# First requests on three queues, and a gate row in four column tiles

## Chip, core and metric

The kernel runs on one core of one Trainium2 chip. The metric is the device time of one execution in microseconds (us). Before the change the median of three runs is 543.81 us (543.6 to 544.0).

The core has TensorE (PE, with its weight loads shown as PEld), VectorE (DVE), ScalarE (ACT), GpSimd (POOL) and SyncE (SP). SP, ACT and POOL can each issue DMA transfers on a queue of their own. Each engine works through its instructions in the order in which the program lists them.

## What is computed

One transformer block on x of 2048 rows and 576 columns, modulated by a condition vector c of 576 values:

```python
mod = (silu(c) @ w_mod).reshape(1, 6, 1, 576)
sa, ca, ga, sb, cb, gb = mod[:, 0], ..., mod[:, 5]
h = layernorm(x) * (1 + ca) + sa
x = x + ga * A(h)       # 32 heads of 18, each row attends to 8 rows, 2 apart, then wo
h = layernorm(x) * (1 + cb) + sb
x = x + gb * ((h @ w_gate) * (h @ w_up)) @ w_down      # 4608 hidden columns
```

The six modulation rows depend on c alone. The rows `ga` and `gb` (here the attention gate row and the MLP gate row) multiply whole columns of the output, so they are needed on all 128 partitions; the other four are needed as columns.

## The kernel before

The 2048 rows are cut into eight chunks of 256. The MLP works on groups of chunks, `[0], [1, 2], [3, 4], [5, 6], [7]`. For each group there is a gate-up loop (36 steps, one per 128 hidden columns, TensorE products `pg` and `pu` at L706) and a down loop (`acc` at L921, `accr` at L926). Attention of the coming chunks is interleaved with these loops. Chunk 0, chunk 1 and part of chunk 2 run ahead of the first gate-up loop, in an opening whose order is written out by hand; this opening lasts about 49 us.

**The opening.** The program asks for the transfers in this order. ACT's queue: `c_row`, the vector c, in three requests (L185, L187). SP's queue: the two halves of chunk 0 of x (L203), the two "tails" of the modulation weights `wmA` (the last 64 of the 576 contraction rows, L190), the two main parts of `wmA` (L206), then the QK and V weights (L174, L175), chunk 1 of x (L136), the weights `wmC` of the attention gate row (L180, L181) and more. TensorE first runs filler matmuls (`keep_busy`, L196: seven of 512 columns), then transposes c (`pc`, L1029), runs seven more fillers, and computes the first two modulation rows as columns (`mod_columns`, L321). These products use four column tiles: four matmuls with 32 columns of weights each write four 32-partition strips of one bank (L328). Between them stand the transposes of the normalised x (L313). ACT copies the result (L332), it is transposed again and added (L342, L345), the transposed x is modulated (L302, L304), and the first QK products follow (L416).

POOL spends the opening on memsets and masks, the identity matrix among them (L221, L222), and issues few transfers.

**The gate rows.** `mod_row` (L349) computes a gate row on all 128 partitions at once: the weights are the condition vector repeated 128 times (`sc_bc`), and five matmuls of 512 columns (`pa`) and five of 64 (`pb`) accumulate over the five parts of the contraction; ACT copies both to an f32 tile. It runs once for the attention gate in the opening (`wmC`) and once for the MLP gate (`gb_row`, L1257) in the first gate-up loop. The weights of the second one are loaded by `load_wm5` (L1015) on POOL's queue, into a spare part of the tile `hh` and a tile `wm5r` from the pool of output tiles (named `o_t` in the profile). `gb_row` then asks on POOL's queue for block 3 of `w_down` (`ld_d1`, L1252, which also lands in a spare part of `hh`). The row is used from the end of the first down loop on, near 127 us (L949, L954, L996).

**The first gate-up loop.** Its weights come in blocks of four steps (`load_wgu`, L154; block 3 is also kept in a spare part of `hh`, so the profile shows it as `hh<-in_B_w_up_dram`). What is interleaved is placed by a planner (`timed`, L808). It gets threads of pieces, each with a cost on TensorE, a cost on DVE, the marks that it needs, the mark that it sets and a delay after which the mark counts; it keeps a clock and puts a piece after the first step at which its marks are due. It also places the QK and V products of chunk 3 as pairs of row tiles (`qkv_of`). Chunk 3's layer norm (`norm_of`, L683) is normalised on ACT (`norm_act`, L283, ACT's work at L287): per half of the chunk one instruction of 576 columns, and one of 64 that repeats the last columns. The chunk is then transposed by DMA on SP's queue (`a_td`, L391, `hT<-xn`) and modulated (`a_mod`).

Of the kernel before, what the change touches and what calls it, by code (L numbers as in the profile page):

```python
# [7 lines left out]
BF = mybir.dt.bfloat16  # L8
# [10 lines left out]
P = 128  # L19
D = 576  # L20
# [6 lines left out]
DIL = 2  # L27
FF = 4608
FT = FF // P
HALO = 16  # L30
SPAN = 14
EPS = 1e-5
# [12 lines left out]
def kernel(  # L45
# [55 lines left out]
    eps = consts.tile([P, 1], F32, name="eps")  # L101
    modc = consts.tile([P, 4, KT], F32, name="modc")
    ga_bc = consts.tile([P, D], F32, name="ga_bc")
    gb_bc = consts.tile([P, D], F32, name="gb_bc")
    sc_bc = consts.tile([P, KT, P], BF, name="sc_bc")
    xns = [consts.tile([P, ST, DP], BF, name=f"xn{k}") for k in range(2)]
    o_sb = consts.tile([P, ST, DP], BF, name="o_sb")
# [5 lines left out]
    wv = wts.tile([P, KT, D], BF, name="wv")  # L113
    wo = wts.tile([P, KT, D], BF, name="wo")
    vd = dramp.tile([HALO + S, D], BF, name="vd")
    prod_t = consts.tile([P, 4 * KT * CH], BF, name="prod_t")
    prod_n = [0]

# [63 lines left out]

    wmA = sp.tile([P, KT, 2 * D], BF, name="wmA")
    c_row = sp.tile([KT, P], BF, name="c_row")
    nc.scalar.dma_start(c_row[0:KF, :], c[0, 0:KF * P].rearrange("(m p) -> m p", p=P))  # L185
    for c0 in (0, 64):
        nc.scalar.dma_start(c_row[KF:KT, c0:c0 + 64], c[:, KF * P:D])  # L187
    def load_wm_tail(wm, blk):
        for b in range(2):
            nc.sync.dma_start(wm[64 * b:64 * (b + 1), KF, b * D:(b + 1) * D], w_mod[KF * P:D, (blk + b) * D:(blk + b + 1) * D])  # L190

    maskneg = sp.tile([P, W, H], BF, name="maskneg")
    busy_w = sp.tile([P, NB], BF, name="busy_w")
# [2 lines left out]
    def keep_busy(n, cols):  # L196
        bank = ps([P, NB], F32, "busy")
        for _ in range(n):
            nc.tensor.matmul(bank[:, 0:cols], lhsT=busy_w[:, 0:P], rhs=busy_w[:, 0:cols], start=True, stop=True)

    x_in[0] = xin.tile([P, ST, D], BF, name="x_t")
    for j in range(ST):
        nc.sync.dma_start(x_in[0][:, j, :], x_flat[js(j), :])  # L203
    load_wm_tail(wmA, 0)
    for k in (0, 2):
        nc.sync.dma_start(wmA[:, k:k + 2, :], w_mod[k * P:(k + 2) * P, 0:2 * D].rearrange("(k p) n -> p k n", p=P))  # L206
    nc.vector.memset(eps[:], EPS)
# [52 lines left out]
    def ln_parts(src, tag, act=False, both=None):  # L260
        stats = small.tile([P, ST, 2, 6], F32, name="ln_stats" + tag)
        mv = small.tile([P, ST, 2], F32, name="ln_mv" + tag)
        rstd = small.tile([P, ST], F32, name="ln_rstd" + tag)
        xn = xns[turn[0] % 2]
        turn[0] += 1
        both = tag == "b" if both is None else both

        def stat(j, hfs=(0, 1)):
            for hf in hfs:
                nc.vector.bn_stats(stats[:, j, hf, :], src(j)[:, hf * 288:(hf + 1) * 288])  # L270
            if hfs[-1] == 1:
# [11 lines left out]
        def norm_act(j):  # L283
            nb = small.tile([P, 1], F32, name="ln_nb")
            nc.vector.scalar_tensor_tensor(nb[:], mv[:, j, 0:1], -1.0, rstd[:, j:j + 1], ALU.mult, ALU.mult)
            for d0, s0, n in ((0, 0, D), (D, D - 64, 64))[0:2 if both else 1]:
                nc.scalar.activation(xn[:, j, d0:d0 + n], src(j)[:, s0:s0 + n], ACTF.Identity, bias=nb[:], scale=rstd[:, j:j + 1])  # L287
        return xn, stat, rsq, (norm, norm_act) if act is None else norm if not act else norm_act

    def layernorm(src, tag, act=False, both=None):  # L290
        xn, stat, rsq, norm = ln_parts(src, tag, act, both)
        for j in range(ST):
            stat(j)

        def norms(js=range(ST)):
            for j in js:
                norm(j)
        return xn, lambda: rsq(slice(0, ST)), norms

    def modulate(dst, s, m, vi_scale, vi_shift, on_dve):  # L300
# [20 lines left out]
    def mod_columns(wm, pi, fill=lambda: None, steps={}):  # L321
        pm = ps([P, 320], F32, "pm")
        order = (KF, 0, 1, 2, 3)
        for kt in order:
            for q in range(4):
                rows = slice(0, P) if kt < KF else slice(64 * (q // 2), 64 * (q // 2) + 64)
                c0 = (q // 2) * D + (q % 2) * 256
                nc.tensor.matmul(pm[H * q:H * (q + 1), :], lhsT=sc_bc[rows, kt, 0:H], rhs=wm[rows, kt, c0:c0 + 320],  # L328
                                 start=(kt == order[0]), stop=(kt == order[-1]), skip_group_check=True)
            steps.get(kt, nop)()  # L330
        mrow = sp.tile([P, 320], BF, name="mrow")
        nc.scalar.copy(mrow[:], pm[:])  # L332
        fill()
        tr = ps([P, 3, P], BF, "pm_t")
        for n in range(2):
            nc.tensor.transpose(tr[:, n, :], mrow[:, n * P:(n + 1) * P], ident[:])
        for r in (slice(0, 64), slice(64, P)):
            nc.tensor.transpose(tr[r, 2, :], mrow[:, 2 * P:], ident[:])
        c01 = slice(2 * pi, 2 * pi + 2)

        def adds():
            nc.vector.tensor_tensor(modc[:, c01, 0:KF].rearrange("p b (u v) -> p b u v", v=2),  # L342
                                    tr[:, 0:2, :].rearrange("p v (b u x) -> p b u v x", b=2, u=2)[:, :, :, :, 0],
                                    addc[:, :, 0:KF].rearrange("p b (u v) -> p b u v", v=2), ALU.add)
            nc.vector.tensor_tensor(modc[:, c01, KF:KT], tr[:, 2, :].rearrange("p (b x) -> p b x", b=2)[:, :, H:H + 1],  # L345
                                    addc[:, :, KF:KT], ALU.add)
        return adds

    def mod_row(wm, dst):  # L349
        pa = ps([P, 512], F32, "pa")  # L350
        pb = ps([P, 64], F32, "pb")
        for p_t, c0, c1 in ((pa, 0, 512), (pb, 512, D)):
            for kt in range(KT):
                m = wm(kt)
                rows = slice(0, m.shape[0])
                nc.tensor.matmul(p_t[:], lhsT=sc_bc[rows, kt, :], rhs=m[:, c0:c1],
                                 start=(kt == 0), stop=(kt == KT - 1))
        nc.scalar.copy(dst[:, 0:512], pa[:])
        nc.scalar.copy(dst[:, 512:D], pb[:])
# [667 lines left out]
    keep_busy(7, NB)  # L1027
    pc = ps([P, KT], BF, "pc")
    nc.tensor.transpose(pc[:], c_row[:], ident[0:KT, 0:KT])  # L1029
# [238 lines left out]
    at = [k for k, p in enumerate(first) if p[3] == "o11"][0] + 2  # L1268
    first[at] = (0.6, 0, "o11", "-", 0, lambda: b_o(1))
    gbg = {0: (qkv_of(3, "p17 z3"),  # L1270
               [[(0, 0, "", "-", 0, lambda: (load_wm5(), load_wd(0))), (0, 0, "", "z3", 8.0, both_halves), (0, 0, "", "w5", 12.0, nop), (1.5, 0, "w5", "-", 0, gb_row), (0, 0, "", "-", 0, lambda: load_res(2))],
                first,
                norm_of(3, "", "", 5) + [(0, 2.5, "", "m4", 0.2, lambda: a_ln(4)), (0, 0, "m4", "r4", 1.0, lambda: aa[4]["rsq"]()),
                                         (0, 0, "r4", "e4", 2.0, lambda: aa[4]["norm"]((0,))), (0, 0, "e4", "n4", 1.6, lambda: aa[4]["norm"]((1,))),
# [85 lines left out]
```

## Time and profile before

| what | value |
|---|---|
| median of three runs | 543.81 us |
| the profiled execution | 544.44 us |
| its span in the profile | 542.7 us |
| TensorE busy | 535.3 us, 99% of the span |
| VectorE, ScalarE, GpSimd busy | 58%, 46%, 13% |
| granted TensorE clock | 1.00 |
| bytes moved | 114.52 MB, 211 GB/s on average |
| DMA rate, 1 to 6 us, each us | 26, 250, 152, 116, 293 GB/s |
| DMA rate, 6 to 10 us, each us | 406, 403, 382, 381 GB/s |

The profile shows one execution, on a clock that starts with the span. The chain of waits follows the work that ended last back to the start: each entry is the instruction or transfer for which the next one waited, or the one before it on the same engine. The timeline lists instructions in order of time: start, duration, engine, line, operation, tile written, tile read, shape, how many were merged. What stands in brackets at the end is the idle time of the engine just before and what ended it; "issue" there means that the profile shows no cause. The starts of TensorE's matmuls are to be trusted more than their ends, which are modelled. Idle time of an engine that is not the bottleneck costs nothing.

### The profile page before, as it was taken

To read this page: it belongs to the slowest core of one execution; us is meant where nothing else is said; L and a number is where in the kernel's file an instruction comes from. 1 tells how busy PE (TensorE), PEld (TensorE's weight loads), DVE (VectorE), ACT (ScalarE), POOL (GpSimd) and SP (SyncE) were. 2 spreads that over 40 slices of the span, in tenths; PEclk is the share of its full clock that TensorE was granted. 3 is DMA by queue.
4 is the path that set the end of the run, shared out by engine and by line. 5 is a ranking of instruction groups with operands and counts; after the bars stand their busy time and mean duration, and the time that the engine had idled before them with its cause. 6 is when DMAs were issued, how large, how long until landed. Compare 5 with 4: busy or idle time off the path is not lost.

```text
span 542.7 us, 14569 instructions
## 1 busy us (share of the span) xinstructions
PE 535.3 (99%) x6157; PEld 321.9 (59%) x6189; DVE 315.9 (58%) x713; ACT 251.5 (46%) x617; POOL 67.9 (13%) x104
## 2 busy tenths in 40 slices
PE   8999999999999999999999999999999999999997
PEld 4887789756745444555544444555544445558875
DVE  4989586777766777646358896524344924032212
ACT  4776777543566553022645552014555551006630
POOL 7104012122000110111000110110010101010210
PEclk9999999999999999999999999999999999999999
DMA  8999999778872694878435983894296592849821
GB/s 264 299 261 363 336 272 332 258 224 258 267 203 89 211 208 153 227 220 293 135 108 163 232 288 68 162 239 159 89 275 176 156 311 69 255 138 294 271 74 42
DMA packets 94924, 114.52 MB, mean 211 GB/s; under 512 B 27980, under 2 KB 83676, under 8 KB 94732
## 3 DMA queue, kind: packets, MB, share of 16 engines
q1 hardware_dynamic: 83360, 67.29, 44.6%
q0 software_dynamic: 11344, 46.25, 27.8%
q8 instruction: 48, 0.79, 0.6%
q14 instruction: 16, 0.13, 0.1%
q10 hardware_dynamic: 156, 0.07, 0.0%
HBM read 103.15 MB, written 4.74 MB: 199 GB/s over the span
## 4 chain that ended last, share of the span: by engine, by line
PE 94%; DMA 3%; DVE 1%; SPq 1%; ACT 1%; issue 0%
PE pg L706 28%; PE pu L706 23%; PE acc L921 19%; PE pq L706 3%; PE accr L926 3%; PE pw L605 3%; PE pq L416 3%; PE acc L976 3%; PE lgT L470 2%; DMA wmC<-in_w_mod_dram 2%; PE pv L706 2%; PE pv L439 1%; DMA wqk<-in_A_wqkv_dram 1%; PE po L567 1%; PE pwj L584 0%
## 5 line engine op out<-in xcount | busy, mean ns | idle before, releaser
L706 PE MATMUL pg<-h2T,wgu 64*128 64x512 bf16 (+1 forms) x1376 | 265.5, 331 | 0.0
L706 PE MATMUL pu<-h2T,wgu 64*128 64x512 bf16 (+1 forms) x1376 | 264.5, 331 | 0.0
L706 PEld LDWEIGHTS <-wgu 64*128 64x128 bf16 x2752 | 136.5, 94 | 94.8 <-issue 0.5
L757 ACT CAST u_sb<-pu 128x512 bf16<-128x512 f32 (+1 forms) x172 | 85.4, 497 | 135.8 <-PE pg L706 131.2
L760 DVE TENSOR_TENSOR hh<-g_sb,u_sb 128x512 bf16<-128x512 bf16 x136 | 57.4, 423 | 116.2 <-ACT g_sb L758 115.7
L758 ACT CAST g_sb<-pg 128x512 bf16<-128x512 f32 (+1 forms) x172 | 86.7, 504 | 0.0
L921 PEld LDWEIGHTS <-hh 128*128 128x128 bf16 x504 | 49.0, 98 | 59.5 <-issue 1.5
L921 PE MATMUL acc<-wd,hh 128*128 128x512 bf16 x329 | 84.1, 380 | 0.1
L926 PE MATMUL accr<-wd,hh 128*128 128x64 bf16 x344 | 62.4, 193 | 0.7
L706 PE MATMUL pu<-h2T,wgr 64*128 64x512 bf16 (+1 forms) x188 | 61.5, 327 | 0.2 <-ACT u_sb L757 0.2
L706 PE MATMUL pg<-h2T,wgr 64*128 64x512 bf16 (+1 forms) x188 | 61.5, 327 | 0.0
L926 PEld LDWEIGHTS <-hh 128*128 128x128 bf16 x504 | 45.8, 98 | 1.9
L171 POOL DMA_DIRECT2D wd<-in_B_w_down_dram x29 | 21.8, 752 | 190.0 <-PE accr L926 93.4
L461 DVE TENSOR_TENSOR prod_t<-qT,kT 128x1280 bf16<-128x1280 bf16 x56 | 43.7, 818 | 0.7 <-ACT kT L777 0.7
L514 DVE TENSOR_TENSOR vsh<-vsh,attn 128x1152 bf16<-128x1152 bf16 x56 | 39.6, 748 | 1.2 <-DMA vsh<-vd 1.2
L706 PEld LDWEIGHTS <-wgr 64*128 64x128 bf16 x376 | 19.7, 94 | 15.4 <-issue 2.5
L921 PE MATMUL acc<-prod_t,hh 128*128 128x512 bf16 x111 | 28.8, 380 | 0.0
L304 ACT ACTIVATE h2T<-h2T,modc 128x256 bf16<-128x256 bf16 x12 | 6.6, 595 | 45.3 <-DMA h2T<-xn 45.3
L455 POOL DMA_DIRECT2D vsh<-vd x14 | 12.5, 897 | 104.8 <-DVE o_sb L524 89.6
L706 PE MATMUL pq<-hT,wqk 64*128 64x256 bf16 (+1 forms) x360 | 22.2, 259 | 0.1
L416 PE MATMUL pq<-hT,wqk 128*128 128x256 bf16 (+1 forms) x225 | 21.2, 251 | 0.4 <-ACT hT L304 0.4
L926 PE MATMUL accr<-prod_t,hh 128*128 128x64 bf16 x112 | 21.6, 193 | 0.1
(208 smaller groups left out, 605.0 us busy)
## 6 DMA issues: line engine op xcount, KB each, us to landing
wgu<-in_B_w_gate_dram SPq DMA_DIRECT2D x41, 512.0 KB, 4.5
wgu<-in_B_w_up_dram SPq DMA_DIRECT2D x41, 512.0 KB, 6.4
wd<-in_B_w_down_dram POOLq DMA_DIRECT2D x29, 576.0 KB, 5.6
vsh<-vd POOLq DMA_DIRECT2D x14, 1152.0 KB, 9.3
prod_t<-in_B_w_down_dram POOLq DMA_DIRECT2D x8, 576.0 KB, 7.6
hh<-in_B_w_down_dram POOLq DMA_DIRECT2D x6, 576.0 KB, 6.4
x_r<-in_A_x_dram SPq DMA_DIRECT2D x8, 288.0 KB, 8.3
vd<-v_sb POOLq DMA_DIRECT2D x16, 144.0 KB, 5.2
```

Of the source, the lines that this page charges most:

```text
L171: return nc.gpsimd.dma_start(wb[:], B_w_down[r0:r0 + FB * P, :].rearrange("(k p) n -> p k n", p=P))
L416: nc.tensor.matmul(pq[:, gi, :], lhsT=wqk[:, kt, m * P:(m + 1) * P], rhs=hT[:, kt, cols], start=(kt == order[0] and not (by_k and gi)), st ...
L461: nc.vector.tensor_tensor(prod, aa[i]["qT"][:], aa[i]["kT"][:, :, off:off + CH], ALU.mult)
L514: nc.vector.tensor_tensor(v, v, at, ALU.mult)
L605: nc.tensor.matmul(pw[:], lhsT=oT[:, m, js(j)], rhs=wo[:, m, 0:512], start=(m == 0), stop=(m == KT - 1))
L706: return nc.tensor.matmul(out, lhsT=lhs, rhs=rhs, start=first, stop=last, skip_group_check=True)
L757: nc.scalar.copy(u[:, c, :], pu)
L758: nc.scalar.copy(g[:, c, :], pg)
L760: return lambda: nc.vector.tensor_tensor(hh[:, f - c:f + 1, :], g, u, ALU.mult)
L921: nc.tensor.matmul(acc[j][:], lhsT=hh[:, f, js(j)], rhs=wb[:, f % FB, 0:512], start=(f == 0), stop=(f == FT - 1))
L926: nc.tensor.matmul(accr[:, j, :], lhsT=hh[:, f, js(j)], rhs=wb[:, f % FB, 512:D], start=(f == 0 and j == 0), stop=(f == FT - 1), skip_grou ...
L976: nc.tensor.matmul(acc[i][:], lhsT=hh[:, f, js(j)], rhs=wb(f)[:, c0:c1], start=(f == 0), stop=(f == FT - 1))
```

## The change

There are three parts.

1. **Opening.** c is requested on POOL's queue (two requests instead of three on ACT's). The second half of chunk 0 of x and the two tails of `wmA` are requested on ACT's queue instead of SP's. The second set of fillers has five matmuls instead of seven.
2. **Normalisation of chunk 3.** The planner gets four pieces (576 and 64 columns of each half, with delays of 1.0, 1.0, 1.0 and 1.6) instead of two (delays 2.0 and 1.6).
3. **MLP gate row.** A new function `gb_cols` computes the row in four column tiles of 144 columns each: 20 matmuls instead of ten, one ACT copy instead of two. The row then lies in four strips; POOL writes it to DRAM and reads it back on all partitions. The row becomes bf16 instead of f32, and the new tile `grow` is as wide as needed to keep the two together at the old size (2304 bytes per partition). The matmuls use all 128 rows for the tail, so the unused half of `wm5r` is set to zero. The planner's cost of the row is 0.85 instead of 1.5.

```diff
+GC = D // 4
+GR = D
...
-    gb_bc = consts.tile([P, D], F32, name="gb_bc")
+    gb_bc = consts.tile([P, D], BF, name="gb_bc")
+    grow = consts.tile([P, GR], BF, name="grow")
...
-    nc.scalar.dma_start(c_row[0:KF, :], c[0, 0:KF * P].rearrange("(m p) -> m p", p=P))
-    for c0 in (0, 64):
-        nc.scalar.dma_start(c_row[KF:KT, c0:c0 + 64], c[:, KF * P:D])
-    def load_wm_tail(wm, blk):
+    nc.gpsimd.dma_start(c_row[0:KF, :], c[0, 0:KF * P].rearrange("(m p) -> m p", p=P))
+    nc.gpsimd.dma_start(c_row[KF:KT, :].rearrange("p (t n) -> p t n", t=2), bass.AP(c.tensor, c.offset + KF * P, [[D, 1], [0, 2], [1, 64]]))
+
+    def load_wm_tail(wm, blk, queue):
...
-    for j in range(ST):
-        nc.sync.dma_start(x_in[0][:, j, :], x_flat[js(j), :])
-    load_wm_tail(wmA, 0)
+    nc.sync.dma_start(x_in[0][:, 0, :], x_flat[js(0), :])
+    nc.scalar.dma_start(x_in[0][:, 1, :], x_flat[js(1), :])
+    load_wm_tail(wmA, 0, nc.scalar)
...
+    def gb_cols(wm):
+        pa = ps([P, GC], F32, "pa")
+        for kt in range(KT):
+            for q in range(4):
+                nc.tensor.matmul(pa[H * q:H * (q + 1), :], lhsT=sc_bc[:, kt, 0:H], rhs=wm(kt)[:, GC * q:GC * (q + 1)],
+                                 start=(kt == 0), stop=(kt == KT - 1), skip_group_check=True)
+        nc.scalar.copy(grow[:, 0:GC], pa[:])
+        nc.gpsimd.dma_start(gd[:], grow[0:P:H, 0:GC])
+        nc.gpsimd.dma_start(gb_bc[:], bass.AP(gd.tensor, gd.offset, [[0, P], [1, D]]))
...
-        norm = [(0, 0, f"r{n}", f"e{n}", 2.0, lambda: aa[n]["norm"]((0,))), (0, 0, f"e{n}", f"n{n}", 1.6, lambda: aa[n]["norm"]((1,)))]
+        norm = [(0, 0, f"r{n}" if k == 0 else f"e{n}{k - 1}", f"e{n}{k}" if k < 3 else f"n{n}", 1.0 if k < 3 else 1.6, lambda k=k: aa[n]["norm"]((k // 2,), (k % 2,)))
+                for k in range(4)]
...
+        nc.gpsimd.memset(wm5r[64:, :], 0.0)
         nc.gpsimd.dma_start(wm5(), w_mod[0:KF * P, 5 * D:6 * D].rearrange("(k p) n -> p k n", p=P))
...
-    keep_busy(7, NB)
+    keep_busy(5, NB)
...
-    load_wm_tail(wmB, 3)
+    load_wm_tail(wmB, 3, nc.sync)
...
-        mod_row(lambda k: wm5()[:, k, :] if k < KF else wm5r[0:64, :], gb_bc)
+        gb_cols(lambda k: wm5()[:, k, :] if k < KF else wm5r[:])
         ld_d1(3)
...
-(0, 0, "", "w5", 12.0, nop), (1.5, 0, "w5", "-", 0, gb_row)
+(0, 0, "", "w5", 12.0, nop), (0.85, 0, "w5", "-", 0, gb_row)
```

More of the change, by code (lines that the diff above doesn't have):

```diff
@@ L115 @@
     vd = dramp.tile([HALO + S, D], BF, name="vd")
+    gd = dramp.tile([4, GC], BF, name="gd")
     prod_t = consts.tile([P, 4 * KT * CH], BF, name="prod_t")
@@ L184 @@
     c_row = sp.tile([KT, P], BF, name="c_row")
-    nc.scalar.dma_start(c_row[0:KF, :], c[0, 0:KF * P].rearrange("(m p) -> m p", p=P))
-    for c0 in (0, 64):
-        nc.scalar.dma_start(c_row[KF:KT, c0:c0 + 64], c[:, KF * P:D])
-    def load_wm_tail(wm, blk):
+    nc.gpsimd.dma_start(c_row[0:KF, :], c[0, 0:KF * P].rearrange("(m p) -> m p", p=P))
+    nc.gpsimd.dma_start(c_row[KF:KT, :].rearrange("p (t n) -> p t n", t=2), bass.AP(c.tensor, c.offset + KF * P, [[D, 1], [0, 2], [1, 64]]))
+    def load_wm_tail(wm, blk, queue):
         for b in range(2):
-            nc.sync.dma_start(wm[64 * b:64 * (b + 1), KF, b * D:(b + 1) * D], w_mod[KF * P:D, (blk + b) * D:(blk + b + 1) * D])
+            queue.dma_start(wm[64 * b:64 * (b + 1), KF, b * D:(b + 1) * D], w_mod[KF * P:D, (blk + b) * D:(blk + b + 1) * D])
     maskneg = sp.tile([P, W, H], BF, name="maskneg")
@@ L281, in norm, with norm_act @@
                                         ALU.subtract, ALU.mult)
[L283 to L286, printed above, removed]
+        nbs = {}
+        def norm_act(j, parts=(0, 1)):
+            if j not in nbs:
+                nbs[j] = small.tile([P, 1], F32, name="ln_nb")
+                nc.vector.scalar_tensor_tensor(nbs[j][:], mv[:, j, 0:1], -1.0, rstd[:, j:j + 1], ALU.mult, ALU.mult)
+            nb = nbs[j]
+            for d0, s0, n in [((0, 0, D), (D, D - 64, 64))[p] for p in parts if p == 0 or both]:
                 nc.scalar.activation(xn[:, j, d0:d0 + n], src(j)[:, s0:s0 + n], ACTF.Identity, bias=nb[:], scale=rstd[:, j:j + 1])
@@ L293, in layernorm, with norms @@
             stat(j)
-        def norms(js=range(ST)):
+        def norms(js=range(ST), *parts):
             for j in js:
-                norm(j)
+                norm(j, *parts)
         return xn, lambda: rsq(slice(0, ST)), norms
@@ L1270 @@
     gbg = {0: (qkv_of(3, "p17 z3"),
-               [[(0, 0, "", "-", 0, lambda: (load_wm5(), load_wd(0))), (0, 0, "", "z3", 8.0, both_halves), (0, 0, "", "w5", 12.0, nop), (1.5, 0, "w5", "-", 0, gb_row), (0, 0, "", "-", 0, lambda: load_res(2))],
+               [[(0, 0, "", "-", 0, lambda: (load_wm5(), load_wd(0))), (0, 0, "", "z3", 8.0, both_halves), (0, 0, "", "w5", 12.0, nop), (0.85, 0, "w5", "-", 0, gb_row), (0, 0, "", "-", 0, lambda: load_res(2))],
                 first,
```

## Prediction

> **What bounds the kernel now.** I read the page first, then the chain of waits, then the timeline of the stretches that the change touches.
>
> ```profile
> span 542.7 us, 14569 instructions
> PE 535.3 (99%) x6157; PEld 321.9 (59%) x6189; DVE 315.9 (58%) x713; ACT 251.5 (46%) x617; POOL 67.9 (13%) x104
> PE 94%; DMA 3%; DVE 1%; SPq 1%; ACT 1%; issue 0%
> ```
>
> TensorE has work in 99% of the span and carries 94% of the chain. It takes its instructions in order, so time removed from its stream counts in full, unless the next thing it waits for does not come earlier too. The 3% DMA and 1% SPq are the places to look; the chain of the first 21 us shows them:
>
> ```profile
> 4.11 6.48 DMA wqk<-in_A_wqkv_dram
> 11.76 8.89 DMA wmC<-in_w_mod_dram
> ```
>
> The first QK weights land at 10.59, the weights of the attention gate at 20.65. Ahead of 4.11 that chain is only SP issuing. The timeline (start, duration, engine, line, what):
>
> ```profile
> 0.82 0.87 SPq L203 DMA_DIRECT2D x_t<-in_A_x_dram  x2
> 1.74 1.19 SPq L190 DMA_DIRECT2D wmA<-in_w_mod_dram  x2
> 2.25 0.68 POOL L226 DMA_DIRECT2D vd<-zrow  x1 [0.30 <-POOL zrow L225]
> 2.97 1.10 SPq L206 DMA_DIRECT2D wmA<-in_w_mod_dram  x2
> 4.11 0.47 SPq L174 DMA_DIRECT2D wqk<-in_A_wqkv_dram  x1
> 4.37 0.18 PE L1029 MATMUL pc<-shifts,c_row 5*128 5x5 bf16 x1
> 4.48 2.68 PE L199 MATMUL busy<-busy_w 128*128 128x512 bf16 x7
> 7.09 0.32 PE L328 MATMUL pm<-wmA,sc_bc 64*32 64x320 bf16 x4
> 10.63 0.10 PEld L416 LDWEIGHTS <-wqk 128*128 128x128 bf16 x1 [0.26 <-DMA wqk<-in_A_wqkv_dram]
> ```
>
> The reader is to see three SP issues ahead of the modulation weights that need not be there, and seven filler matmuls between the transpose of c (4.37) and the first useful product (7.09).
>
> The last stretch is the MLP gate row, in the first gate-up loop:
>
> ```profile
> 57.40 1.20 ACT L287 ACTIVATE xn<-x_t,ln_nb,ln_rstda 128x576 bf16<-128x576 bf16 x2
> 58.91 0.85 PEld L706 LDWEIGHTS <-wgu 64*128 64x128 bf16 x16 [0.46 <-issue]
> 62.71 1.04 PE L356 MATMUL pa<-hh,sc_bc 128*128 128x512 bf16 x3
> 63.67 0.39 PE L356 MATMUL pa<-o_t,sc_bc 64*128 64x512 bf16 x1
> 63.99 0.29 PE L356 MATMUL pb<-hh,sc_bc 128*128 128x64 bf16 x4
> 64.63 0.33 PEld L706 LDWEIGHTS <-hh 64*128 64x128 bf16 x7 [0.28 <-DMA hh<-in_B_w_up_dram]
> ```
>
> A normalisation of 1.20 us on ACT holds back an eviction and so TensorE (0.46); the row takes ten matmuls; and right behind it TensorE waits for a weight block (block 3, kept in a spare part of hh). The table of DMA issues says how late two transfers land (us, last column):
>
> ```profile
> hh<-in_B_w_up_dram SPq DMA_DIRECT2D x1, 512.0 KB, 22.9
> hh<-in_B_w_down_dram POOLq DMA_DIRECT2D x1, 576.0 KB, 12.4
> ```
>
> The first is issued at 41.67 and lands at 64.6; the second, issued at 52.86, lands at 65.3, so they share the DMA engines.
>
> **Part 1, the opening.** SP loses three issues (one half of x, two weight tails), so its issue of wmA moves from 2.97 to 1.28, by 1.69 us, and all behind it as well. The moved bytes (144 + 2x72 KB) must still flow; at the 400 GB/s of the seconds after 6 us they take 0.74. So data come about 0.9 us earlier, wqk at about 9.7. I use 0.9, bounds 0 and 1.69. ACT now issues x's other half and the tails: three issues of 0.41, 0.56 and 0.59 from 0.82 on end near 2.5, its table load (1.28) near 3.75; its first work starts at 4.09, so this costs nothing, and up to 1 us if the table load slid further. The tails then land (2.4 after issue) near 4.3, needed near 6.6.
>
> POOL now begins with two issues of c. The nearest row is its 0.68 us issue of zrow, landing 2.2 after its start: c arrives at 0.82+0.68+2.2 = 3.7. The fillers ahead of the transpose end near 4.3 (seven at 0.43 from 1.27), so it is hidden by 0.6; past that each late us costs one, since all of PE's queue stands behind the transpose. POOL's memsets and the mask of the transpose move back by 1.4, the mask to 2.8; the copy of sc_bc at 11.51 moves to 12.9, needed at 20. Nothing waits for them. The Trainium skill, "DMA: Bandwidth & Descriptors", Specifications, speaks against this move: it gives a first byte after about 1 us from the gpsimd queue against 0.6 from the sync and scalar ones. By that c would come 0.4 later than from ACT's queue, which the fillers would still cover.
>
> Two fillers fewer: their starts lie 0.43 apart until about 6.6, where the later ones speed up, so the last two were cheap. Five end at 6.6, and the first product starts at 6.65 instead of 7.09: 0.45. sc_bc is ready at 5.83, the normalised x at 6.30, needed at 6.9. A gap at 8.60 to 8.88, which I take for wmA's second half, closes by about 0.15. So the first QK product moves from 11.09 to about 10.5, behind its data (9.7). At 20.65 the 0.2 wait for wmC goes as its data come 0.9 earlier. **Opening: -0.75, bounds 0 and -1.1.**
>
> **Part 2, the split normalisation.** ACT's 1.20 becomes a piece of about 0.87 (a single one at 79.00 takes that) and a small one a step later, so the held eviction starts 0.33 earlier. **-0.3, bounds 0 and -0.46.** The constant for the bias is computed once, as before.
>
> **Part 3, the gate row.** Removed: five 512-column and five 64-column matmuls, 62.77 to 64.42 in the chain, 1.65 us. Added: 20 matmuls of 144 columns in four column tiles. No row has that size: 20 of 256 columns in four tiles (L470) take 0.66, 20 with 32 columns (L1076) take 0.49. I take 0.55. **-1.1, bounds -1.0 and -1.2.** ACT copies 144 columns (0.27 by its 128-column casts) instead of 0.58 + 0.22; hidden either way. A DVE product with the gate row in bf16 keeps its price: with one f32 operand 128x512 takes 0.69 (L954, L495), and the other operand remains f32. At most 17 of them fall towards 0.42 (an all-bf16 add, L997), of which TensorE waits only at three group ends (1.3 in all): 0 to -1. The memset of wm5r (0.59 by L231) falls into POOL's wait before 50.77; else wm5r lands 0.6 later than 61.0, needed near 61.7.
>
> POOL gains a write of the row to DRAM, a wait for it, and a broadcast read. Queued behind is the load of w_down block 3, issued at 52.86 now, which then comes only near 67 (ACT's copy near 62.9, 3.4 to 6 us for a small write as for vd). Its user is the down loop past 100 us, and POOL's next issue stands at 79.17: no cost. But it leaves the DMA engines free before 64.6. From wd's landing at 63.2 on the two shared them, so block 3 of w_up gains half of 1.4 us, 0.7; bounds 0 and 1.7 (its 576 KB at 340 GB/s).
>
> The planner's cost of the row falls from 1.5 to 0.85. Followed through its arithmetic, the row stays after step 11 and the normalisation pieces follow steps 6 to 9; the modulation of chunk 3 moves from after step 17 to 18, and its five QK pairs and first V pair come one step later. That gives TensorE 1 us more before it needs hT, for which it waits 0.2 now.
>
> **The sum.** Without new waits: -0.75 - 0.3 - 1.1 = -2.15. TensorE would then want block 3 at 64.37 - 2.15 = 62.2. It lands at 64.6 - 0.8 - 0.7 = 63.1. So TensorE waits 0.9 there where it waited 0.28, and starts at 63.15 instead of 64.64: **-1.5**. Later blocks (68.1, needed 68.4 now) lose 0.8 + 1.7 of queue and keep up; what is late next is hT, priced at zero and bounded in the last rival. After that, transfers are released by TensorE's progress and shift with it. The profiled execution took 544.44 (span 542.7 and 1.74 around it), which becomes 542.9; it lies 0.6 above the median of 543.81, which becomes **542.3**.
>
> **Rivals.**
> - *All arrives in time* (16%): removing w_down from the queue frees the full 1.7. For it: all its bytes now pass before 65.3. Against: part passes after 64.6. -2.2: 541.6.
> - *Block 3 does not move* (13%): its 512 KB take 22.9 us, so something other than bytes ahead may set it. Then TensorE waits 2.4 at 64.6, all gains before are lost: 543.8, no change.
> - *Warm-up comes later* (6%): the fillers' spacing halves only near 6.6, and the useful products now start there. Should the fast rate begin a microsecond or two later in an execution, the 1.6 us of work before the copy of the modulation would double, and -0.75 becomes +0.85. Block 3's wait then shrinks, since -0.55 remains: 543.3. The Trainium skill, "TensorE: Matmul & The Clock Gate", Part 1, says that the window behind this is free-running, about 3.4 us, so the point varies by execution; the trace shows one execution, 5.3 us from the first filler. By that rule alone 543.3 would be seen in some executions.
> - *The displaced load hits the transposes of hT* (17%; slower): they are issued at 65.08 and 67.03 and take 5.2 to land, DVE waits 1.4 for them and TensorE 0.2. Moved to about 67, w_down's load now meets them. They would land at 70.8, and TensorE needs the result near 72.6 with 1.4 us of modulation before. Half the rate for the 576 KB costs 1.7, which the slack swallows but for 0.5. Should it double the 5.2 of both (+3.5), the wait is 3.1: 543.81 - 1.5 + 3.1 = 545.4. It decides from a landing past 74 on. Against: only one transfer of 1.7 us stands in the way.
>
> **How the numbers follow.** The forecast has 48%, its own range 541.7 to 543.2. A measurement here tells 0.2% (1.1 us) from no change. Of the 48, 36 lie beyond it; with the first rival 52% faster. 12 + 13 + 6 = 31% same; 17% slower. The range from 541.0 (full sum plus the bound of the bf16 products in part) to 544.8 leaves out the slower rival and a little below.
>
> **What would show it.** Right: the first pm product near 6.65; wqk landing below 10; 20 short pa products in about 0.55; a wait for hh<-in_B_w_up near 1 us at about 63; the QK pair of chunk 3 without a wait. Wrong: pc later than 4.4, a landing of block 3 that stays at 64.6, a longer wait of DVE for hT, or o_t products other than 0.69.

## The result

The changed kernel takes 548.44 us (median of 6 runs, 546.29 to 549.63) against 543.83 (543.60 to 544.09): a ratio of 1.0074, 95% interval 1.0060 to 1.0088. It is slower; 542.3 was forecast, with a range of 541.0 to 544.8. Its profiled execution took 546.42, one of the two quickest of the six. The medians lie 4.6 us apart and the two profiled executions (544.44 and 546.42) only 2.0: that of before is 0.6 above its median, and 2 us have to be looked for elsewhere. The page of the changed kernel:

```profile
span 544.4 us, 14591 instructions
PE 533.7 (98%) x6166; PEld 320.8 (59%) x6197; DVE 317.2 (58%) x713; ACT 250.9 (46%) x616; POOL 70.9 (13%) x109
PE 95%; DMA 2%; DVE 1%; ACT 1%; issue 0%; SPq 0%
```

TensorE works 1.6 us less (533.7 for 535.3), yet the span is 1.7 us longer: 3.3 us of new idle time. The waits of TensorE name most of it: 3.4 us for `c_row`. The timeline of the opening after the change:

```profile
1.28 0.93 SPq L210 DMA_DIRECT2D wmA<-in_w_mod_dram  x2
2.25 0.47 SPq L178 DMA_DIRECT2D wqk<-in_A_wqkv_dram  x1
1.27 1.17 ACTq L194 DMA_DIRECT2D wmA<-in_w_mod_dram  x2
1.36 0.67 POOL L189 DMA_DIRECT2D c_row<-in_c_dram  x1 [0.83 <-POOLq L1364]
2.01 0.56 POOL L190 DMA_DIRECT2D c_row<-in_c_dram  x1
7.85 0.16 PE L1049 MATMUL pc<-shifts,c_row 5*128 5x5 bf16 x1 [3.40 <-DMA c_row<-in_c_dram]
10.06 0.45 PE L336 MATMUL pm<-wmA,sc_bc 64*32 64x320 bf16 x4
14.52 1.67 PE L434 MATMUL pq<-hT,wqk 128*128 128x128 bf16 x27 [0.43 <-DMA wv<-in_A_wqkv_dram]
```

The transpose of c (`pc`) stands at 7.85 instead of 4.37, the first modulation product at 10.06 instead of 7.09, the first QK product at 14.52 instead of 11.09. (The last bracket names `wv`, which this product does not read; for the same gap the profiles of e2, e13 and e14 name ACT's `hT`, as that of before does.) The DMA issues of the first 16 us (KB each, us from issue to landing):

```profile
c_row<-in_c_dram POOLq DMA_DIRECT2D x1, 1.0 KB, 4.8
c_row<-in_c_dram POOLq DMA_DIRECT2D x1, 0.2 KB, 5.7
wmA<-in_w_mod_dram ACTq DMA_DIRECT2D x2, 72.0 KB, 5.4
vd<-zrow POOLq DMA_DIRECT2D x1, 18.0 KB, 6.4
wqk<-in_A_wqkv_dram SPq DMA_DIRECT2D x1, 576.0 KB, 8.4
```

In the kernel before, the tails took 2.4 and `zrow` 2.2. SP did issue wmA and wqk 1.7 to 1.9 us sooner, but wqk lands at 2.25 + 8.4 = 10.65 where it landed at 4.11 + 6.5 = 10.6: the first QK weights come no sooner, and c, the tails and `zrow` come later. The normalisation of x starts later too, at 3.74 instead of 2.99. Stretches of the opening, before and then after (columns: stretch, its length, busy us and instructions of the engines, granted clock, DMA share, GB/s):

```profile
2.00:4.00 2.00, 2.00 (x6) 0.59 (x4) 0.97 (x4) 1.24 (x1) 1.70 (x3) 1.00 0.74 201
4.00:6.00 2.00, 2.00 (x7) 0.68 (x6) 1.86 (x10) 1.59 (x6) 1.91 (x6) 1.00 0.80 205
```

```profile
2.00:4.00 2.00, 2.00 (x6) 0.60 (x4) 0.26 (x1) 1.28 (x1) 1.64 (x5) 1.00 0.89 285
4.00:6.00 2.00, 0.44 (x2) 0.00 (x0) 1.69 (x7) 0.50 (x2) 1.95 (x4) 1.00 1.05 357
8.00:10.00 2.00, 2.00 (x6) 0.50 (x5) 1.65 (x5) 1.32 (x4) 1.86 (x5) 0.52 1.11 324
```

Before, the DMA engines were not yet full (0.74, 0.80) while c, x and the tails landed; after, they are (1.05 between 4 and 6 us), and in that stretch TensorE, waiting for 1.2 KB, works 0.44 of 2 us. Once it resumes, its granted clock is at half for about 3 us.

The gate row does what was intended. The timeline after:

```profile
65.84 0.43 PE L361 MATMUL pa<-hh,sc_bc 128*32 128x144 bf16 x16
66.10 0.24 PE L361 MATMUL pa<-o_t,sc_bc 128*32 128x144 bf16 x4
66.27 0.28 PE L725 MATMUL pg<-h2T,wgr 64*128 64x256 bf16 x1
```

The ordinary gate-up products go on 0.43 us after the row starts, and block 3's own, at 66.39, without a wait.

One table sorts all profiles. The first down product is where `acc` starts; from there to the end each execution takes 446.3 to 446.9 us, so all is decided before it. Four stretches lead there: the start to the first QK product (pq), on to the first gate-up product (pg), on to the gate row, on to acc. All numbers are starts, or differences of starts, in us.

| profiled execution of | pq | pq to pg | pg to row | row to acc | time |
|---|---|---|---|---|---|
| before | 11.09 | 37.74 | 13.88 | 35.40 | 544.44 |
| the change | 14.52 | 37.55 | 13.77 | 33.72 | 546.42 |
| e4, only c on POOL | 10.99 | 37.55 | 13.87 | 34.71 | 543.60 |
| e2, only the opening | 14.41 | 37.55 | 13.87 | 34.72 | 547.03 |
| e3, change with c on ACT | 15.95 | 37.55 | 13.76 | 36.88 | 550.49 |
| e8, change with doubled requests | 12.04 | 37.67 | 13.76 | 37.86 | 547.96 |
| e1, row and norm | 11.70 | 37.55 | 13.76 | 39.41 | 548.73 |
| e7, the same | 11.06 | 37.94 | 13.77 | 36.08 | 545.19 |
| e5, w_down block 3 ahead | 11.32 | 37.56 | 13.76 | 35.24 | 544.18 |
| e6, block 3 between | 11.18 | 37.55 | 13.77 | 38.25 | 547.06 |
| e11, row alone | 11.25 | 38.13 | 13.87 | 35.09 | 544.64 |
| e9, row and norm, loads deferred | 11.37 | 38.06 | 13.76 | 33.69 | 543.19 |
| e10, loads deferred alone | 11.24 | 37.55 | 13.87 | 34.72 | 543.67 |
| e13, change with loads deferred | 15.64 | 37.55 | 13.77 | 33.70 | 547.38 |
| e12, the change again | 14.54 | 37.56 | 13.77 | 33.73 | 546.42 |
| e14, the change again | 14.93 | 37.55 | 13.76 | 33.69 | 546.75 |
| e15, the change again | 14.70 | 37.55 | 13.77 | 39.01 | 551.85 |

The last stretch has a floor: 34.7 with the old row, 33.7 with the new one. What lies above it goes with a wait, or with a slower clock after one. So row and norm are worth 1.0 + 0.1 us where nothing waits, and the opening costs 3.4. The change itself is at the floor in three of its four profiles, with all its loads in place; e1 and e7, with the same row and norm but the old opening, are not.

### The profile page after: what moved, and what is told of

Its sections match the earlier page's. It is cut to its first block, busy times and chain, and to the rows that moved or that the text cites. A ratio compares the mean times of both kernels' runs of the same rounds, so it can differ in the third digit from the quotient of the medians.

```text
span 544.4 us, 14591 instructions
## 1 busy us (share of the span) xinstructions
PE 533.7 (98%) x6166; PEld 320.8 (59%) x6197; DVE 317.2 (58%) x713; ACT 250.9 (46%) x616; POOL 70.9 (13%) x109
## 4 chain that ended last, share of the span: by engine, by line
PE 95%; DMA 2%; DVE 1%; ACT 1%; issue 0%; SPq 0%
PE pg L725 28%; PE pu L725 23%; PE acc L940 19%; PE pq L434 4%; PE pq L725 3%; PE accr L945 3%; PE pw L623 3%; PE acc L995 3%; PE pv L725 2%; PE pv L457 2%; PE lgT L488 2%; DMA wqk<-in_A_wqkv_dram 2%; PE po L585 1%; DMA wv<-in_A_wqkv_dram 1%; PE pwj L602 0%; PE accr L998 0%
```

## Experiments, first question: why the opening is late

Theory D: the bulk requests (wmA, wqk) were moved ahead, fill the DMA engines, and hold up every small transfer, on whichever queue. Theory Q: POOL's queue brings c late by itself. Each set ran beside the kernel before on its chip, whose medians were 544.46 (e1 to e4), 544.15 (e5 to e8), 544.0 (e9 to e12) and 543.84 (e13 to e15).

**e2: the opening alone**, with the old norm and the old row.

```diff
-        gb_cols(lambda k: wm5()[:, k, :] if k < KF else wm5r[:])
+        mod_row(lambda k: wm5()[:, k, :] if k < KF else wm5r[0:64, :], gb_bc)
```

> The changed opening alone, with the old normalisation and the old gate row. Both theories: the transpose of c waits until near 7.8 us, the first QK product starts near 14.5 instead of 11.1, and the time is that of after plus the 1.2 to 1.7 us that the other parts save: 547.5 to 550.5.

Measured: 547.32 (546.86 to 547.87), ratio 1.0055 (1.0040 to 1.0070); `pc` at 7.83. The opening alone makes the kernel slower; the time lies just under the range expected.

**e4: before, with nothing but c on POOL's queue.**

```diff
-    nc.scalar.dma_start(c_row[0:KF, :], ...)
+    nc.gpsimd.dma_start(c_row[0:KF, :], ...)
```

> The kernel before with one edit: c requested on POOL's queue. SP's requests stand where they stood. Theory Q: c lands 5 to 6 us after its issue as in after, near 7.5, TensorE waits 3 us: 546.5 to 548. Theory D: the DMA engines are as free as in before, c lands 2.2 us after its last issue, near 4.3 as zrow did, and the time is within 0.5 us of before.

Measured: 543.93 (543.60 to 547.30), ratio 0.9994 (0.9979 to 1.0010). Its DMA issues:

```profile
c_row<-in_c_dram POOLq DMA_DIRECT2D x1, 1.0 KB, 2.3
c_row<-in_c_dram POOLq DMA_DIRECT2D x1, 0.2 KB, 2.3
```

The same two requests on the same queue, issued at 1.35 and 2.01 as in the change, land in 2.3 us instead of 4.8 and 5.7. Theory Q falls. `zrow`, which now goes out at 4.01, behind the bulk, takes 5.0 instead of 2.2.

**e3: the whole change, c back on ACT's queue, first in it.**

```diff
-    nc.gpsimd.dma_start(c_row[0:KF, :], ...)
+    nc.scalar.dma_start(c_row[0:KF, :], ...)
```

> The whole change, but c is requested first on ACT's queue as before, ahead of the half of x and the tails. Theory Q (POOL's queue is late by itself, 5.7 us from issue): c lands near 4.3, the transpose starts at 4.4, and the time is at or below that of the run with before's opening, 541.5 to 542.6. Theory D (the requests for weights that were moved 1.7 us ahead keep the DMA engines busy, and small transfers on any queue wait for them): c is issued at 0.82 to 1.7 beside them and lands between 4.5 and 6.5; 542.5 to 545.

Measured: 548.0 (547.29 to 550.49), ratio 1.0075 (1.0048 to 1.0102). `pc` now starts at 5.17, but what stands behind c on ACT is late instead. Its DMA issues, then VectorE's timeline:

```profile
x_t<-in_A_x_dram ACTq DMA_DIRECT2D x1, 144.0 KB, 5.4
wmA<-in_w_mod_dram ACTq DMA_DIRECT2D x2, 72.0 KB, 5.8
```

```profile
7.41 0.82 DVE L275 BATCH_NORM_STATS2 ln_statsa<-x_t 128x6 f32<-128x288 bf16 x2 [3.27 <-DMA x_t<-in_A_x_dram]
```

The second half of x takes 5.4 us (2.2 before), VectorE waits 3.27 for it, and the condition vector `sc_bc`, queued behind that on VectorE, is late for TensorE: QK at 15.95. Another queue, the same loss. The time misses both theories, for neither asked what would wait in c's place. (The profiled execution is the longest of the four and lost 3.2 us more between row and acc.)

**e8: the whole change, with copies of the three removed requests back on SP**, into a buffer that nobody reads. They add 288 KB and move the bulk back to 2.97; c stays on POOL, x's half and the tails on ACT.

```diff
+    dup = sp.tile([P, 3, D], BF, name="dup")
+    nc.sync.dma_start(dup[:, 0, :], x_flat[js(1), :])
+    for b in range(2):
+        nc.sync.dma_start(dup[64 * b:64 * (b + 1), 1 + b, :], w_mod[KF * P:D, b * D:(b + 1) * D])
     for k in (0, 2):
         nc.sync.dma_start(wmA[:, k:k + 2, :], ...)
```

> The whole change, and on SyncE's queue the three small requests that the change took off it are put back as copies that go to an unused buffer, ahead of the modulation weights, so that the bulk requests start at about 2.97 as in before while c stays on GpSimd's queue and the tails and half of x on ScalarE's. Theory D (the bulk weight requests, moved ahead by 1.7 us, hold up every small transfer): c is transposed at 4.3 to 5, first QK product at 10.6 to 11.6 instead of 14.5, first gate-up product (pg) near 49, in all 3 us below the changed kernel, 542.5 to 545.5. Theory Q (the new queues themselves are late): c at about 7.8, QK at 14 or later, 546 or more.

Measured: one execution, 547.96. Its DMA issues and its timeline:

```profile
c_row<-in_c_dram POOLq DMA_DIRECT2D x1, 1.0 KB, 3.2
c_row<-in_c_dram POOLq DMA_DIRECT2D x1, 0.2 KB, 2.9
```

```profile
5.04 0.16 PE L1053 MATMUL pc<-shifts,c_row 5*128 5x5 bf16 x1 [0.60 <-DMA c_row<-in_c_dram]
```

In the opening theory D holds: more bytes to move and the same queues, and QK comes at 12.04, 2.5 us sooner than in the change, though 0.4 outside what was expected. c's landing time follows the traffic: 2.3 us (bulk at 2.97), about 3.1 (bulk at 2.97 and 288 KB of copies), 4.8 and 5.7 (bulk at 1.28). The total missed D's range and lies in Q's, because this execution lost 4.2 us between row and acc. That is the second question.

The Trainium skill, "Trainium Kernel Development and Optimization", Key Constraints, says that the queues of SP, ACT and POOL run on the same 16 DMA engines and interleave, so that issuing from several of them saves only issue time. e2, e3 and e8 agree, and add the price: the issue time saved here, 1.7 us, came with a loss of 3.4.

## Experiments, second question: where the row's 1.1 us go

Theory W: the load of w_down block 3, which POOL now issues near 72 instead of 53 us because it queues behind the row's trip through DRAM, runs into the weight blocks of the gate-up loop. Theory B: up to about 96 us the DMA engines are as fully taken as TensorE, so time saved on TensorE comes back as a wait for something that lands no sooner. Theory V: the planner's new order makes the pauses, whatever the loads.

The row of DMA busy tenths on the page of before, one digit for each 13.6 us, speaks for B:

```profile
DMA  8999999778872694878435983894296592849821
```

Seven digits of 8 and 9 in a row, the first 95 us: just the stretch in which the change saves time. Nowhere later are there so many.

**e1 and e7: the opening of before, with the split norm and the new row** (one kernel, run twice).

```diff
-    keep_busy(5, NB)
+    keep_busy(7, NB)
...
-    nc.gpsimd.dma_start(c_row[0:KF, :], ...)
+    nc.scalar.dma_start(c_row[0:KF, :], ...)
...
-    nc.scalar.dma_start(x_in[0][:, 1, :], x_flat[js(1), :])
-    load_wm_tail(wmA, 0, nc.scalar)
+    nc.sync.dma_start(x_in[0][:, 1, :], x_flat[js(1), :])
+    load_wm_tail(wmA, 0, nc.sync)
```

> The opening of before, with the split normalisation and the new gate row kept. Both theories put the whole loss into the opening, so both expect a gain here: 42 instead of 165 hundredths of a microsecond for the row (after's trace: 65.84 to 66.26) and 0.3 for the normalisation, 1.2 to 1.7 us in all, 542.1 to 542.6. If the wait for block 3 of w_up grows as predicted, 542.6 or a little above; if not, 542.2. A rival, that the row's way through DRAM costs something later, expects 543.8 or more.

> The same kernel as e1_row_and_norm, looked at once more for a profile of its common execution near 543.8. Theory W: the chain from 74 to 98 us holds one or more waits for a w_gate or w_up block, 1 us or more in all, with acc near 98. Theory V: no such wait, and acc near 98 all the same, by pauses of TensorE spread over the stretch.

Measured: e1 543.89 (543.46 to 548.73, 11 runs), ratio 0.9992 (0.9982 to 1.0001), where 542.1 to 542.6 was expected; e7 545.19. Most of the 1.1 us does not arrive, as the rival said that expected 543.8 or more. TensorE's waits in the loop of e7:

```profile
PE pu L726 <- DMA wgu<-in_B_w_up_dram: 1.4, 1, 1.4
PE pq L726 <- ACT qT L795: 0.5, 1, 0.5
```

And in e1's profiled execution, the longest of its eleven:

```profile
83.83 0.39 PE L726 MATMUL pu<-h2T,wgu 64*128 64x256 bf16 x1 [2.60 <-DMA wgu<-in_B_w_up_dram]
```

Both wait for a weight block, which W and B say and V does not.

**e11: the row alone**, with the old norm and the old opening.

```diff
-        norm = [... for k in range(4)]
+        norm = [(0, 0, f"r{n}", f"e{n}", 2.0, lambda: aa[n]["norm"]((0,))), (0, 0, f"e{n}", f"n{n}", 1.6, lambda: aa[n]["norm"]((1,)))]
```

> Before with the new gate row alone (old norm, old opening). Theory B: the row saves 1.1 us at 63 us and the loop gives it back in waits for weight blocks or transposes, 0.998 to 1.001 of before. Rival: the split norm's longer list of planned steps, not the row, makes the waits; then the row alone keeps its 1.1 us, 0.998 or less, with no wait over 0.3 us between 64 and 97.

Measured: 544.51 (543.09 to 546.20), ratio 1.0004 (0.9990 to 1.0018), with a wait of 1.0 us for a w_up block. The longer list of planned steps is not the cause.

**e5 and e6: block 3 of w_down issued sooner**, on top of e1: ahead of the row's two transfers (e5, the diff), or one line lower, between them (e6).

```diff
         nc.scalar.copy(grow[:, 0:GC], pa[:])
+        ld_d1(3)
         nc.gpsimd.dma_start(gd[:], grow[0:P:H, 0:GC])
         nc.gpsimd.dma_start(gb_bc[:], ...)
...
-        ld_d1(3)
```

> The opening of before with the split norm and the new gate row; the load of w_down block 3 is issued ahead of the row's two transfers, so at about 53 us as in before, not at 72. Theory W (the displaced load of w_down block 3 runs into the w_gate and w_up blocks and the transposes of 66 to 90 us, and that takes back the 1.2 us which norm and row save): no wait of TensorE for a w_gate or w_up block between 75 and 95 us, first partial of the down loop (acc) near 97.0 to 97.4 against 98.1 in before, but the block 3 of w_up again lands near 64.3 while TensorE wants it near 63.1, a wait of about 1 us, so 543.2 to 543.6 in all. Rival V (the gain is lost to the planner's new order or to TensorE itself, whatever the loads): 543.7 to 544.1, acc at 98.0 or later with no wait for block 3.

> As the one before, but the load of w_down block 3 is issued between the write of the row and its broadcast read, so at about 64 us: behind the landing of block 3 of w_up and ahead of the w_gate and w_up blocks that collide with it at 72. Theory W: no wait for block 3 of w_up and none for the later blocks; acc near 96.9, 542.5 to 542.8. Theory V: 543.7 to 544.1. The rival of the prediction (the load beside the two transposes of hT issued at 65 and 67 holds up chunk 3's products): a wait of TensorE for hT of 0.5 to 3 us near 72 to 75, 543.5 to 546.

Measured: e5 545.64 (543.82 to 546.84), ratio 1.0018 (1.0001 to 1.0034); e6 545.0 (544.38 to 547.10), ratio 1.0015 (1.0000 to 1.0030). Both missed the times given for W and for V; e6 met those of the prediction's rival. The profile of e5 shows one of its quicker executions (544.18), so what makes its median of 545.64 was not seen. It starts block 3 of w_up without a wait at 63.19, and later shows this (waits of TensorE in e5, then in e6):

```profile
PE pq L727 <- ACT qT L796: 0.9, 1, 0.9
```

```profile
PE pq L727 <- DVE hT L311: 2.1, 1, 2.1
```

Wherever the load is put within the loop, something else waits: a w_up block, the eviction of a QK pair (in e7 and e5), or the transposes of hT (in e6, with the load issued at 64.8). W is too narrow: the place of this load alone does not decide it. What is left to test is the sum of the loads.

**e9: e1 with the loads of w_down blocks 3 and 4 taken out of the loop** (1.15 MB); block 3 is issued once the loop's last gate-up block has landed (91.05), block 4 at 94.92. **e10: the same deferral on the kernel before**, as the control.

```diff
-... (0, 21): lambda: ld_d1(4), ...
+... (0, 21): nop, ...
...
-    first.insert(at + 4, (0, 0, "v2", "-", 0, lambda: behind(b_ld(2, 0), wgu_in[8])))
+    first.insert(at + 4, (0, 0, "v2", "-", 0, lambda: (behind(ld_d1(3), wgu_in[8]), b_ld(2, 0))))
...
-        a4 = [(0, 0, "", "h4", 1.5, lambda: ld_prods(0))]
+        a4 = [(0, 0, "", "h4", 1.5, lambda: (ld_d1(4), ld_prods(0)))]
```

> As e1_row_and_norm (before's opening, split norm, new gate row), and the loads of w_down blocks 3 and 4 (1.15 MB, about 3.4 us of the DMA engines at 340 GB/s) are taken out of the first gate-up loop: block 3 is issued behind the landing of the last w_gate block, near 93 us, block 4 near 97. Theory B (between 12 and 96 us the DMA engines are as fully taken as TensorE, so that TensorE's saved 1.2 us come back as waits for blocks and transposes that land no earlier): no wait of TensorE over 0.3 us between 63 and 97, acc near 96.5 to 97, in all 0.9975 to 0.9985 of before, 542.7 to 543.2. Rival L (the waits come from the latency of the transposes and the planner's order, bytes or not): waits of 1 us or more remain between 70 and 96, 0.999 to 1.003. Rival V2: block 3, 4 or the shifted values then come late to the down loop, a wait of 1 to 3 us between 100 and 115 us and 544 to 546.

> Before with nothing but the two w_down loads deferred in the same way: the control of e9. Theory B: before has no wait over 0.3 us between 63 and 98 that the loads could cause, so nothing is gained, 0.9985 to 1.0005 of before, and e9 lies 0.7 to 1.2 us below this kernel. Rival L: the same here, and e9 not below this kernel by more than 0.3 us.

Measured: e9 542.86 (542.36 to 543.73, 12 runs), ratio 0.9976 (0.9966 to 0.9985); e10 543.68 (543.55 to 546.48, 12 runs), ratio 0.9998 (0.9987 to 1.0008). Both fall where theory B put them, e9 by 0.8 us below its control and the only version here that beats before. Stretches of e7, then of e9:

```profile
60.00:72.00 12.00, 11.84 (x242) 9.69 (x239) 8.69 (x17) 9.17 (x30) 1.96 (x3) 1.00 1.15 291
72.00:84.00 12.00, 11.51 (x215) 10.54 (x213) 10.99 (x25) 9.51 (x30) 2.24 (x3) 1.00 1.05 256
84.00:96.00 12.00, 10.61 (x181) 9.57 (x179) 6.56 (x12) 8.48 (x23) 1.76 (x3) 1.00 1.02 338
```

```profile
60.00:72.00 12.00, 11.85 (x241) 9.90 (x241) 8.97 (x19) 9.19 (x30) 1.18 (x2) 1.00 1.13 295
72.00:84.00 12.00, 12.00 (x233) 11.00 (x227) 10.65 (x24) 9.91 (x33) 1.51 (x2) 1.00 0.90 246
84.00:96.00 12.00, 12.00 (x212) 11.04 (x209) 8.05 (x14) 9.67 (x27) 4.95 (x8) 1.00 1.02 321
```

The first number behind the length is TensorE's busy time: 11.51 and 10.61 in e7, 12.00 and 12.00 in e9. The last but one is the DMA share: 1.05 between 72 and 84 in e7, 0.90 in e9. e9 has no wait over 0.2 us left in the loop. So taking the two loads out brings the row's gain. What they did there is less clear: the rate hardly differs between 72 and 84 (256 and 246 GB/s), the bytes and the two requests went together, and which of them counts was not separated. B also leaves out why the change reaches its floor with the loads in place; that its TensorE, 3 us late, gives the loads time is argued only, and e3, later still, waits 2.9 us.

## Experiments, third question: the rest of the median

**e12, e14, e15: the changed kernel, profiled again; e13: the change with the deferral of e9.**

> The whole change once more, for a profile of one of its executions near 548 to 549; the profile at hand shows one of 546.4. Theory B with D: the opening as in the profile at hand (QK at 14.5), and 1.5 to 3 us more of waits for weight blocks or transposes between 65 and 97 us. Rival: the opening itself varies, QK later than 15.5, and nothing later differs by more than 0.5 us. If the execution is again one of 546 to 547, this run tells nothing.

> The whole change, to catch an execution of 548 or more in a profile. Theory B: QK at 14.5 as in the profiles at hand, and waits for blocks or transposes of 1.5 us or more between 63 and 97. Rival O: QK later than 15.5 and the loop as in the profiles at hand. An execution near 546.4 tells nothing.

> As the look before it, a further chance to see such an execution; the same numbers.

> The whole change, with the loads of w_down blocks 3 and 4 deferred as in e9. The two profiles at hand of the whole change show executions of 546.4 without a wait in the loop of 63 to 97 us, while most of its executions took 548 to 549.6. Theory B (the rest are executions in which that loop waits for blocks or transposes): with less to transfer there the waits go, and all executions fall together at 545.5 to 546.6, 1.003 to 1.0045 of before. Rival O (the opening itself varies from one execution to the next): the spread stays, median 547.5 to 549, 1.006 to 1.009.

Measured: e12 546.42 and e14 546.75, which tell nothing more; e15 551.85; e13 547.27 (546.17 to 547.44, 6 runs), ratio 1.0054 (1.0040 to 1.0067). e15 caught a long execution. Its waits of TensorE from 60 us on, and its DMA issues between 74 and 96 us:

```profile
PE pu L725 <- issue: 3.4, 1, 3.4
```

```profile
wgu<-in_B_w_gate_dram SPq DMA_DIRECT2D x2, 512.0 KB, 8.9
wgu<-in_B_w_up_dram SPq DMA_DIRECT2D x2, 512.0 KB, 13.5
lg_t<-lgs SPq DMA_TRANSPOSE x1, 14.6
```

Its opening is that of the other executions (QK at 14.70). From 86.75 to 90.18 it waits for 3.4 us, and from 90 to 94 its granted clock is 0.57. The profile names no cause of the wait. I take it for the w_up block issued at 76.72, which took 14.1 us; in the execution of 546.42 the same block took 6.8, and the transpose 8.1 instead of 14.6. The w_gate block just ahead of it took 5.9 and 5.7. Four microseconds of e15, then of the execution of 546.42:

```profile
86.00:90.00 4.00, 0.75 (x13) 0.47 (x8) 0.36 (x1) 0.49 (x2) 0.00 (x0) 1.00 0.89 137
```

```profile
86.00:90.00 4.00, 4.00 (x74) 4.00 (x72) 2.56 (x5) 2.56 (x8) 0.00 (x0) 1.00 1.06 349
```

With the deferral no execution of e13 reached 547.5, where four of the first six of the change lay above 548. That speaks for waits in the loop as this part of the loss, but not for B's reason: while e15 waits, its DMA engines move 137 GB/s, not the 349 of the quick execution. Such a dip is no peculiarity of e15. Every profile has one between 66 and 96 us, a microsecond at 101 GB/s or less; in before it is 17 GB/s between 74 and 75, just after a DMA transpose was issued at 73.67, and e15's lies within the 14.6 us of its transpose. So the DMA engines are full by the average of a stretch, and not in every microsecond of it. That the transposes make the dips is a rival that no run tests.

The opening varies too, as the rival said, and e13's 547.27 lies between the two ranges: QK at 14.41 to 14.93 in five profiles, 15.64 in that of e13. The products of the modulation in e13:

```profile
11.97 0.72 PE L336 MATMUL pm<-wmA,sc_bc 128*32 128x320 bf16 x8
13.17 0.72 PE L336 MATMUL pm<-wmA,sc_bc 128*32 128x320 bf16 x8
```

In the profile of the change both rows take 0.46. c comes 0.2 later in e13, but from the first modulation product to QK it needs 5.23 us instead of 4.46: TensorE goes on at the slow rate for longer.

## Why the prediction was wrong, by its steps

- **Opening, -0.75: this is the step that failed**, and its bounds (0 and -1.1) left a loss out. "Landing 2.2 after its start: c arrives at 3.7" took the landing time of `zrow` for a property of the request. It belongs to the traffic: `zrow` was issued at 2.25 in before, ahead of the bulk at 2.97. With the bulk at 1.28 c took 4.8 and 5.7, `pc` came at 7.85, and the 0.6 of cover was gone: +3.43 at QK where -0.6 was expected. "Past that each late us costs one" held by balance: 3.48 late at `pc`, 3.43 at QK. The two fillers saved 0.51 (0.45 expected) and wmA's gap 0.16 (0.15), but the slow clock after the wait took 0.62 back: the first two sets of modulation products start 1.54 apart instead of 0.92.
- **"wqk at about 9.7"** failed as well: 10.65. The 576 KB took 8.4 us instead of 6.5: with the DMA engines full from 4 us on, what SP issued sooner only queued there. With wqk at 10.6, QK could not have started before that in any case, so the opening had hardly 0.5 to win: e4, quick throughout, has QK at 10.99.
- **c 0.4 later from POOL's queue**, which the prediction weighed and took for covered, did not matter: e4 equals before.
- **Norm, -0.3**: 0.11 (13.88 to 13.77). Right in sign, too large; what else made up the wait of 0.46 was not tried.
- **Row, -1.1**: right. Row and gap 1.66 became 0.55, and the floor from row to acc fell by 1.0.
- **bf16 products, counted at nothing**: right. From acc on all kernels take the same time.
- **Block 3 of w_up, a wait of 0.9**: it did not come in the change, which is 3 us late there, nor in e1, e5, e6, e7 or e9, which want the block at 63.0 to 63.8; of all profiles with the new row only e8 has one (1.3 us).
- **The displaced w_down load, "no cost"**: wrong, though its place alone does not tell: e5 and e6 put it elsewhere and gained nothing. It goes out at 71.0 in e7 and 73.6 in the change, not near 67. Its user is indeed past 100 us, but the step asked only who waits for the load, not what the load keeps from landing. e9 against e1 shows the price of this load and block 4's together: most of the row's gain.
- **The planner's one step** was right: from block 3's products (from 64.64, behind its wait, in before) to the QK pair of chunk 3, 8.5 us became 9.5 in the change.
- **The last rival** (w_down load against the transposes of hT, 545.4, 17%) named a kind of wait that e6 showed, and the right direction; in the change (e15) it seems to have been a weight block. Its price does not add up: a doubling of 5.2 adds 5.2 and not 3.5, and its own numbers leave a slack of 0.4, so that 1.7 would leave a wait of 1.3 and not 0.5.
- **The warm-up rival** (6%) was right as a mechanism and no part of the loss in the change's own profile: the fast rate does come later in some executions, and in e13, next to the profile of the change, that cost 0.77 us against 1.6 in the rival.
- **The sum.** Parts 2 and 3 alone, with two loads deferred, end at 542.86. That this is near the forecast is luck: the forecast counted a gain from the opening and took 0.65 off for a wait that did not come. The opening turned the sign.

What stays open: why the DMA engines move only about 150 GB/s in e15 from 83 to 91, and less than that for shorter times in every profile; and what decides in which execution TensorE's fast rate comes later. That every execution of the change above 548 has a wait like e15's is argued from the spread of e13, not seen in each.

## What to carry to other kernels

A landing time read from a trace holds for the traffic of that trace: before a bulk request is moved ahead, list the small ones that are still in flight and who waits for them, for here a request on any of the three queues was late (e2, e3). Where TensorE and the DMA engines are both nearly full in a stretch, look at what lands there before a saving on TensorE is counted; here the row's 1.1 us arrived, with the old opening, only once 1.15 MB had been moved behind the loop. And where the runs spread over more than one profile shows, profile again before explaining the median.

## What the runs showed of the hardware

A wait can cost more than its length. In the change TensorE's weight loads stop for 4.28 us (3.5 to 7.8), and its granted clock is 0.55, 0.50, 0.50 and 0.75 in the microseconds from 8 to 12, then 1.00; the useful work in that time lost 0.62 us. In e6, where it was busy for 1.9 us of the four from 72 to 76, the clock was 0.56 and 0.59 in the next two stretches of 2 us; after e7's wait of 1.39 us it stayed at 1.00. The clock column is no full witness at the start: for e13 it reads 1.00 from 0 to 24, though both sets of eight products take 0.72 until 13.9 and 0.46 in the change. The Trainium skill, "TensorE: Matmul & The Clock Gate", Part 1, gives a free-running window of about 3.4 us and half clock after an idle one; the traces of the change and of e6 agree in the length, with about 3.4 us at half clock each. No wholly idle window was needed in e6, where TensorE paused for only 2.08 us. The prediction cited the rule but never asked it what a late c would cost.

A request of 1 KB on POOL's queue took 2.3, 3.2 or 4.8 us to land, with nothing changed but what the other queues had in flight.
